# A first unit of 254 tokens, a load on ScalarE's queue and a new order of the steps, in a fused attention and gated feed-forward kernel

## The chip, the core and the metric

One NeuronCore of a Trainium2 chip runs the whole program. The metric is the time of one execution on the device in microseconds (us), the median of several runs. Engines are named as the profile names them: PE is TensorE (the matrix engine; PEld its loads of stationary operands), ACT is ScalarE, DVE is VectorE, POOL is GpSimd, SP is SyncE, which here only starts transfers (DMAs).

## The reference

Chunked attention over 64-token chunks, followed by a feed-forward layer with a depthwise convolution over three neighbouring tokens as its gate. B=8, H=8, S=576, D=64, so the model width is 512; the inner width is 1024.

```python
scores = scale * q_c @ k_c.T            # inside each chunk of 64 tokens
attn = exp(scores - max(scores)); attn = attn / (sum(attn) + 1e-09)
x = (attn @ v_c)  ->  (B, S, 512)
h = maximum(x @ w_in, 0)                # (B, S, 1024)
conv_out[s] = cw[0] * h[s-1] + cw[1] * h[s] + cw[2] * h[s+1]   # zero beyond a sequence's ends
out = (h * sigmoid(conv_out)) @ w_out
```

q, k and v are float32; w_in, conv_w and w_out are float64.

## The kernel before, in words

The tokens of all sequences stand in one line of 4608. Attention works on 36 tiles of 128 tokens (two chunks each), the feed-forward on 16 units, two for each sequence of 576 tokens: 288 and 288.

Attention of a tile t (function `att`): load q and k (`load_rows` for tiles 0 to 8, in groups of three tiles after that), load v, turn q and k so that the head dimension lies on the partitions (`t_pe`, two steps on PE, each copied out of PSUM by ACT in `t_copy`), the scores (PE), row maximum and subtraction (DVE), exponential (ACT), row sum and reciprocal (DVE), the scaling (POOL, `s_norm`), turning the probabilities (`p_pe` on PE, `p_copy` on ACT), the product with v (`attn_v`), and the result split into a rounded part `x_h` (ACT) and the rest `x_l` (DVE). For tiles below `NP` = 5 a row of `load_rows` carries two tokens and is 512 bytes long, and a `t_pe` step is eight matmuls at line 177; for tiles 5 to 8 a row is one token of 256 bytes and a step is four transposes at line 182. Tiles 0 to 8 share two places for their rows (`qk_103` and `qk_104` in the order below), and from tile 12 on the turning of q, k and the probabilities is done without PE.

Feed-forward of a unit u: eight blocks f of 128 inner columns. `mm1` (line 360) multiplies x with w_in in three products (x_h by the rounded weights, x_l by the rounded weights, x_h by the rest), 12 matmuls that stream the unit's tokens plus the neighbours that the convolution needs (290 columns). Then ACT takes the ReLU (`h_relu`) and the middle tap (`c_mid`), DVE adds the outer taps, ACT the tanh (`c_sig`), DVE the product, ACT the rounded part (`g_hi`) and POOL the rest (`g_lo`). `mm2` (line 414) is for an output tile t of 128 tokens and a block f: three matmuls of 512 columns; eight of these steps make a tile, which ACT copies out (`o_copy`) and SP stores (`o_store`). A unit's `mm1` needs x of every attention tile that its tokens touch: unit 0 with 290 columns needs tiles 0, 1 and 2. An output tile needs all units that it touches.

The float64 weights are split on the chip: `w_load` brings a quarter of a matrix (or half of that) into one of two places (`w_105`, `w_106`), then `w_scale` (ACT), `w_shift` and `w_words` (DVE; after these the place is free), `w_hi` (ACT), and `w_left_g` (POOL). A block of `mm1` needs the pieces of its two f, an `mm2` step those of its f.

What runs when is written out: every step is recorded with an engine, a cost and its buffers, `order_` is a list of step numbers, a small planner gives each step a start by its booked cost, and the steps are emitted by that start. Each engine runs its instructions in that order, and waits only for data and buffers. In front of PE steps with an early start the kernel puts filler matmuls on `ident` (lines 926 and 929), which compute nothing that is used; how many is worked out from `pe_free`, the time that the planner books for each filler, and `SLACK`.

```python
while idle and pe_free + (2.0 if pe_free < 5.0 else 1.0) < begin[i] - SLACK:
    nc.tensor.matmul(banks[idle[-1]], lhsT=ident, ...)        # 128x512
```

## Time and profile before

| | |
|---|---|
| runs | 492.12 us median of three (491.23 to 492.7) |
| the profiled execution | 490.69 us, of which the span from first to last instruction is 488.9 us |
| busy, share of the span | PE 98%, DVE 70%, ACT 61%, POOL 39% |
| first `mm1` matmul, last `mm2` matmul on PE | 31.60 us, 485.11 us |
| first `mm2` matmul | 57.82 us |
| moved by DMA | 50.16 MB |

The page gives busy times, the span in 40 slices with a digit for the busy tenths of each, the chain of work that ended last, groups of instructions, and DMA issues. Idle time of an engine costs only where the chain runs through it. Matmuls overlap, so the mean duration of one is longer than the distance between two starts; where the text gives the cost of a matmul it is the distance.

### The profile page before, as it was taken

Reading aid. Unit: us, or ns where it says so; the run is one execution under the profiler, and the core shown is the slowest. Engines: PE = TensorE matmul, PEld = TensorE weight load, DVE = VectorE, ACT = ScalarE, POOL = GpSimd, SP = SyncE. Lnnn points to the kernel's source line nnn. Section 1 sums busy time; section 2 is a strip of 40 time slices with the busy share of each in tenths; the row PEclk is TensorE's granted clock in tenths of the full one; section 3 lists DMA queues with packets and bytes.
Section 4 is the critical chain, followed back from the end, with each engine's and each line's share of the span. In section 5 each row is a group of like instructions: output and inputs, shape, how many; then the busy total and the mean of one; then the engine's idle time right before and its main releaser. Section 6 shows DMA issues by size and latency. Waiting matters only on the chain.

```text
span 488.9 us, 12846 instructions
## 1 busy us (share of the span) xinstructions
PE 478.4 (98%) x4961; PEld 425.2 (87%) x4961; DVE 342.6 (70%) x726; ACT 299.2 (61%) x749; POOL 192.0 (39%) x261
## 2 busy tenths in 40 slices
PE   7799999999999999999999999999999999999996
PEld 4689899989899889898898999998889899998885
DVE  3789988767877788888778687978786655563300
ACT  4589997667564656765556566655654566565411
POOL 1245565252351635355242525352523155143120
PEclk9899999999999999999999999999999999999999
DMA  8998955234655744266565444547302002010012
GB/s 214 297 271 214 269 96 81 48 49 89 131 114 112 147 84 98 47 143 131 101 132 101 100 79 76 118 95 165 82 23 83 24 6 66 0 44 1 21 66 86
DMA packets 180610, 50.16 MB, mean 103 GB/s; under 512 B 164653, under 2 KB 172869, under 8 KB 180549
## 3 DMA queue, kind: packets, MB, share of 16 engines
...
q14 instruction: 23, 0.18, 0.1%
...
## 4 chain that ended last, share of the span: by engine, by line
PE 90%; DMA 4%; ACT 2%; DVE 2%; POOL 1%; issue 1%; SPq 0%; POOLq 0%; ACTq 0%
PE b_ps L414 42%; PE b_ps L360 39%; DMA qk<-in_k 3%; PE sx_ps L309 2%; PE sx_ps L226 2%; PE b_ps L177 2%; PE z_ps L309 1%; DMA w<-in_moe_w_out 1%; PE z_ps L226 1%; PE b_ps L295 1%; DVE wt L456 1%; POOL wi_l L460 1%; ACT wt L447 0%; ACT c L372 0%; SPq L121 0%
## 5 line engine op out<-in xcount | busy, mean ns | idle before, releaser
L405 POOL TENSOR_TENSOR g_l<-c,g_h 128x288 fp32r<-128x288 f32 (+8 forms) x184 | 110.1, 620 | 184.9 <-ACT g_h L401 155.6
L414 PE MATMUL b_ps<-wo_h,g_h 128*128 128x512 f32 x288 | 115.6, 402 | 0.0
L414 PE MATMUL b_ps<-wo_h,g_l 128*128 128x512 f32 x288 | 113.6, 394 | 0.0
L414 PE MATMUL b_ps<-wo_l,g_h 128*128 128x512 f32 x288 | 113.4, 394 | 0.0
L376 DVE SCALAR_TENSOR_TENSOR c<-b_ps,cw,c 128x287 f32<-128x287 f32 (+1 forms) x128 | 64.7, 509 | 55.1 <-ACT c L372 54.7
L360 PE MATMUL b_ps<-x_h,wi_h 128*128 128x290 f32 x512 | 90.3, 298 | 0.2 <-ACT qkT L195 0.2
L360 PE MATMUL b_ps<-x_l,wi_h 128*128 128x290 f32 x512 | 89.6, 297 | 0.0
L367 ACT ACTIVATE b_ps<-b_ps 128x290 f32<-128x290 f32 x128 | 50.8, 399 | 63.1 <-PE b_ps L360 62.8
L360 PE MATMUL b_ps<-x_h,wi_l 128*128 128x290 f32 x512 | 89.2, 296 | 0.0
L360 PEld LDWEIGHTS b_ps<-x_h,wi_h 128*128 128x128 f32 x512 | 80.2, 189 | 9.2 <-ACT qkT L195 0.4
L391 DVE SCALAR_TENSOR_TENSOR c<-c,b_ps 128x288 f32<-128x288 f32 x128 | 56.7, 446 | 35.7 <-ACT c L388 35.2
L388 ACT ACTIVATE c<-c 128x288 f32<-128x288 f32 x128 | 56.6, 444 | 41.0 <-DVE c L382 40.1
L360 PEld LDWEIGHTS b_ps<-x_l,wi_h 128*128 128x128 f32 x512 | 75.8, 190 | 0.0
L360 PEld LDWEIGHTS b_ps<-x_h,wi_l 128*128 128x128 f32 x512 | 75.4, 189 | 0.0
L372 ACT ACTIVATE c<-b_ps,cw 128x288 f32<-128x288 f32 x128 | 63.9, 501 | 9.7 <-POOL g_l L405 2.4
L382 DVE SCALAR_TENSOR_TENSOR c<-b_ps,cw,c 128x288 f32<-128x288 f32 (+1 forms) x128 | 64.8, 512 | 2.8
L414 PEld LDWEIGHTS b_ps<-wo_h,g_l 128*128 128x128 f32 x288 | 54.2, 188 | 12.7
L401 ACT CAST g_h<-c 128x288 fp32r<-128x288 f32 (+8 forms) x184 | 58.3, 355 | 7.1 <-PE b_ps L414 3.6
L414 PEld LDWEIGHTS b_ps<-wo_h,g_h 128*128 128x128 f32 x288 | 54.4, 189 | 8.6
L414 PEld LDWEIGHTS b_ps<-wo_l,g_h 128*128 128x128 f32 x288 | 54.2, 188 | 7.5
L271 POOL TENSOR_TENSOR wt<-wt,z 128x512 f32<-128x512 f32 x24 | 25.3, 1053 | 45.9 <-DVE z L262 18.6
L419 ACT ACTIVATE wt<-b_ps 128x512 f32<-128x512 f32 x36 | 21.4, 597 | 31.2 <-PE b_ps L414 31.1
...
## 6 DMA issues: line engine op xcount, KB each, us to landing
out<-wt SPq DMA_DIRECT2D x36, 256.0 KB, 2.4
v<-in_v SPq DMA_DIRECT2D x21, 256.0 KB, 3.5
...
wt<-wt SPq DMA_DIRECT2D x48, 64.0 KB, 2.0
...
```

The lines of the kernel that those rows point to most:

```text
L271: nc.gpsimd.tensor_tensor(out=two(st, "to"), in0=two(st, "of"), in1=z, op=ALU.mult)
L360: nc.tensor.matmul(h_ps[:, 0:hi - lo], lhsT=wt[:, f // 2, kt, P * (f % 2):P * (f % 2) + P], rhs=xt[:, u % NX, kt, 0:hi - lo], start=n == 0 ...
L367: nc.scalar.activation(out=h, in_=h, func=AF.Relu)
L372: nc.scalar.mul(out=st["c"], in_=banks[st["h"]][:, i0:i0 + st["n"]], mul=cw[:, FT + f:FT + f + 1])
L376: nc.vector.scalar_tensor_tensor(out=c[:, a:n], in0=banks[st["h"]][:, i0 + a - 1:i0 + n - 1], scalar=cw[:, f:f + 1], in1=c[:, a:n], op0=AL ...
L382: nc.vector.scalar_tensor_tensor(out=c[:, 0:b], in0=banks[st["h"]][:, i0 + 1:i0 + 1 + b], scalar=cw[:, 2 * FT + f:2 * FT + f + 1], in1=c[: ...
L388: nc.scalar.activation(out=st["c"], in_=st["c"], func=AF.Tanh, scale=0.5)
L391: nc.vector.scalar_tensor_tensor(out=st["c"], in0=st["c"], scalar=1.0, in1=banks[st["h"]][:, st["i0"]:st["i0"] + st["n"]], op0=ALU.add, op ...
L401: nc.scalar.copy(out=g_h[:, f, gs], in_=st["c"][:, cs])
L405: nc.gpsimd.tensor_tensor(out=g_l[:, f, gs], in0=st["c"][:, cs], in1=g_h[:, f, gs].bitcast(F32), op=ALU.subtract)
L414: nc.tensor.matmul(banks[st["o"]], lhsT=gt[:, f, o:o + P], rhs=wt[:, f, :], start=f == 0 and n == 0, stop=f == FT - 1 and n == 2)
L419: nc.scalar.mul(out=st["os"], in_=banks[st["o"]], mul=0.5)
```

## The change

- **Units.** The first sequence is cut into 254 and 322 tokens instead of 288 and 288; the other sequences stay. Unit 0 then streams 256 columns and needs attention tiles 0 and 1 alone; unit 1 streams 324. `x_h` and `x_l` get slots of differing length (`x_slot`), the buffer `c` is longer. Output tile 1 (tokens 128 to 255) now touches units 0 and 1.
- **Loads.** `NP` = 7: tiles 5 and 6 are loaded two tokens to a row and turned by the eight matmuls. Tile 0's q and k are issued from ACT's queue, ahead of ACT's table load.
- **The last output tile** is made in two halves of 256 columns, each with its own eight `mm2` steps, copy and store.
- **Filler.** A filler is booked with 1.5 and then 0.9 us instead of 2.0 and 1.0, `SLACK` is 0.3 instead of 0.7, PE counts as free from 1.4 us.
- **Buffers.** `e` has two buffers instead of three.
- **The list** `order_` is a new one.

```diff
-    CUTS0 = [0, HS]
-    XU = HS + 2
-    XS = XU + 2
+    FIRST = 2 * P - 2
+    CUTS0 = [0, FIRST]
+    NC_ = S - FIRST
     NX = 3
+    XS = [HS + 4, NC_ + 2, HS + 4]
...
-    SLACK = 0.7
-    NP = 5
+    SLACK = 0.3
+    NP = 7
...
-                    nc.sync.dma_start(out=r[i, p0:p0 + n], ...)
+                    (nc.sync if t else nc.scalar).dma_start(out=r[i, p0:p0 + n], ...)
...
-        st["e"] = work3.tile([P, H, C], F32, name="e")
+        st["e"] = work.tile([P, H, C], F32, name="e")
...
+    def x_slot(x, u):
+
+        o = KT * sum(XS[0:u % NX])
+        return x[:, o:o + KT * XS[u % NX]].rearrange("p (k i) -> p k i", k=KT)
...
-    def mm2(st, t, f):
+    def mm2(st, t, f, m=slice(0, DM)):
...
-            nc.tensor.matmul(banks[st["o"]], lhsT=gt[:, f, o:o + P], rhs=wt[:, f, :],
+            nc.tensor.matmul(banks[st["o"]][:, m], lhsT=gt[:, f, o:o + P], rhs=wt[:, f, m],
...
+            cuts = [(slice(0, DM),), ] if t < NT - 1 else [(slice(0, DM // 2),), (slice(DM // 2, DM),)]
...
-        0, 30, 12, 72, 91, 31, 32, 33, 13, 1, 14, 77, 15, 73, 16, 36, 74, 75, 2, 4, 17, 3, 92, 76, 110, 5, 6,
...
-    pe_free, until_ = 2.0, 110.0
+    pe_free, until_ = 1.4, 110.0
+    ahead = next(i for i in order_ if steps[i]["fn"] is load_rows)
+    steps[ahead]["fn"](*steps[ahead]["args"])
+    nc.scalar.activation(out=rebias, in_=ident[:, 0:1], func=AF.Exp)
+    nc.gpsimd.memset(rebias, -896.0 * 2 ** 23)
...
-            while idle and pe_free + (2.0 if pe_free < 5.0 else 1.0) < begin[i] - SLACK:
+            while idle and pe_free + (1.5 if pe_free < 5.0 else 0.9) < begin[i] - SLACK:
```

How the order moves is shown at three places. A row is a line, an operation, the tile written and those read, and a count.

First PE, from the middle of the start-up to the first `mm1`. L177 (after: L176) is `t_pe`, L226 (L225) the scores, L295 (L294) `p_pe`, L309 (L308) the product with v, L360 (L364) `mm1`, L929 (L941) filler, L507 the turning of conv_w. Before:

```order
L177 MATMUL b_ps<-ident,qk_104 64x128 x8
L295 MATMUL b_ps<-ident,e 128x128 x4
L309 MATMUL sx_ps<-pT,v 64x64 x32
L507 MATMUL b_ps<-ident,wt 128x24
L177 MATMUL b_ps<-ident,qk_103 64x128 x8
L295 MATMUL b_ps<-ident,e 128x128 x4
L226 MATMUL sx_ps<-qkT 64x64 x16
L309 MATMUL sx_ps<-pT,v 64x64 x16
L177 MATMUL b_ps<-ident,qk_103 64x128 x8
L929 MATMUL b_ps<-ident 128x128
L360 MATMUL b_ps<-x_h,wi_h 128x290 x4
```

and after, the same engine and place:

```order
L294 MATMUL b_ps<-ident,e 128x128 x8
L941 MATMUL b_ps<-ident 128x128 x2
L225 MATMUL sx_ps<-qkT 64x64 x16
L308 MATMUL sx_ps<-pT,v 64x64 x16
L176 MATMUL b_ps<-ident,qk_101 64x128 x16
L308 MATMUL sx_ps<-pT,v 64x64 x16
L176 MATMUL b_ps<-ident,qk_102 64x128 x16
L364 MATMUL b_ps<-x_h,wi_h 128x256 x4
```

Before, tile 2's `p_pe` and product with v stand ahead of the first `mm1`; after, those of tiles 0 and 1 alone do, but both `t_pe` steps of tiles 4 and 5 (`qk_101`, `qk_102`), of which tile 5's stood behind it before.

Second the start of the loads, on SP (before):

```order
L434 DMA w_105<-in_moe_w_in 128x2x512
L434 DMA w_106<-in_moe_w_in 128x2x512
L121 DMA qk_103<-in_q 64x8x128
L121 DMA qk_103<-in_k 64x8x128
L121 DMA qk_104<-in_q 64x8x128
L121 DMA qk_104<-in_k 64x8x128
L434 DMA w_105<-in_moe_conv_w 24x256
```

and after, SP's queue (tile 0 is issued by ACT):

```order
L438 DMA w_103<-in_moe_conv_w 24x256
L120 DMA qk_102<-in_q 64x8x128
L120 DMA qk_102<-in_k 64x8x128
L438 DMA w_104<-in_moe_w_in 128x2x512
L438 DMA w_103<-in_moe_w_in 128x2x512
L120 DMA qk_101<-in_q 64x8x128
L120 DMA qk_101<-in_k 64x8x128
```

Tiles 0 and 1 now go ahead of the first two half pieces of w_in, which went ahead of them before; the last two rows are tile 2.

Third SP at the first pieces of w_out, up to the second of them, which holds blocks 0 and 1 and with that what the first `mm2` step needs. Before:

```order
L434 DMA w_105<-in_moe_w_in 128x4x512
L128 DMA qk_104<-in_q 128x8x64
L128 DMA qk_104<-in_k 128x8x64
L434 DMA w_106<-in_moe_w_out 128x2x1024
L167 DMA v<-in_v 128x4x64
L167 DMA v<-in_v 64x4x64 x2
L434 DMA w_105<-in_moe_w_out 128x2x1024
```

and after:

```order
L438 DMA w_103<-in_moe_w_in 128x4x512
L166 DMA v<-in_v 128x4x64
L166 DMA v<-in_v 64x4x64 x2
L438 DMA w_104<-in_moe_w_out 128x2x1024
L127 DMA qk_102<-in_q 128x8x64
L127 DMA qk_102<-in_k 128x8x64
L166 DMA v<-in_v 64x4x64 x4
L438 DMA w_103<-in_moe_w_out 128x2x1024
```

Ahead of that second piece stood q and k of tiles 0 to 5 and v of tiles 0 to 3; now q and k of tiles 0 to 7 and v of tiles 0 to 4, two tiles of 0.52 MB and one v of 0.26 MB more. Behind the first `mm2` step PE now has blocks of `mm1` of units 1 and 2 where steps of output tile 1 stood, since that tile waits for unit 1.

More of the change, by code (lines that the diff above doesn't have):

```diff
@@ L90, in attn_ffn @@
     rebias = const.tile([P, 1], F32, name="rebias")
-    nc.scalar.activation(out=rebias, in_=ident[:, 0:1], func=AF.Exp)
-    nc.gpsimd.memset(rebias, -896.0 * 2 ** 23)
     wi_h = const.tile([P, FT // 2, KT, 2 * P], F32R, name="wi_h")
@@ L97, in attn_ffn @@
     wo_l = const.tile([P, FT, DM], F32R, name="wo_l")
-    x_h = const.tile([P, NX, KT, XS], F32R, name="x_h")
-    x_l = const.tile([P, NX, KT, XS], F32R, name="x_l")
+    x_h = const.tile([P, KT * sum(XS)], F32R, name="x_h")
+    x_l = const.tile([P, KT * sum(XS)], F32R, name="x_l")
     g_h = const.tile([P, FT, GR], F32R, name="g_h")
@@ L553, in att @@
             r = "wslot" if t in W_ROWS else "slot"
[L554 removed]
+            ld = step("SP", 0.02 if t == 0 else 1.2 if (2 * t) % NCK < NCK - 1 else 2.3, load_key, load_rows, (st, t), take=[(r, st)], lag=1.8 if t < NP else 2.6)
             tt = []
@@ L721, in attn_ffn @@
         for i, t in enumerate(outs_in[u] if u <= NU - 1 else []):
-            st = {}
+            cuts = [(slice(0, DM),), ] if t < NT - 1 else [(slice(0, DM // 2),), (slice(DM // 2, DM),)]
             prev = None
-            for f in range(FT):
-                key = U[u + 1] + (U[u + 2] - U[u + 1]) * (i + f / FT) / len(outs_in[u]) + 0.3
-                units = [v_ for v_ in range(NU) if UNITS[v_][0] < P * t + P and P * t < UNITS[v_][1]]
-                prev = step("PE", 0.7, key, mm2, (st, t, f), [prev] + wo_done[f] + [g_done[v_, f] for v_ in units],
-                            take=[("bk", st, "o")] if f == 0 else [])
-                mm2_of[t, f] = prev
-            s = step("ACT", 0.6, key + 1, o_copy, (st,), [prev], take=["wt"], free=[("bk", "o")])
-            step("SP", 0.5, key + 2, o_store, (st, t), [s], free=["wt"], lag=0.8)
+            for n, m in enumerate(cuts):
+                st, w = {}, 1.0 / len(cuts)
+                m = m if w < 1.0 else ()
+                for f in range(FT):
+                    key = U[u + 1] + (U[u + 2] - U[u + 1]) * (i + f / FT) / len(outs_in[u]) + 0.3 + 3.0 * n
+                    units = [v_ for v_ in range(NU) if UNITS[v_][0] < P * t + P and P * t < UNITS[v_][1]]
+                    prev = step("PE", 0.018 + 0.682 * w, key, mm2, (st, t, f) + m, [prev] + wo_done[f] + [g_done[v_, f] for v_ in units],
+                                take=[("bk", st, "o")] if f == 0 else [])
+                    mm2_of[t, f] = prev
+                s = step("ACT", 0.18 + 0.42 * w, key + 1, o_copy, (st,) + m, [prev], take=["wt"], free=[("bk", "o")])
+                step("SP", 0.5, key + 2, o_store, (st, t) + m, [s], free=["wt"], lag=0.8 * w)
     early = {"DVE": 0.083, "ACT": 0.092, "PE": 0.0, "POOL": -0.075, "SP": -0.05}
@@ L932, in attn_ffn @@
         n = len(nc.cur_bb.bb.instructions) if steps[i]["port"] else 0
-        steps[i]["fn"](*steps[i]["args"])
+        if i != ahead:
+            steps[i]["fn"](*steps[i]["args"])
         if steps[i]["port"]:
```

27 lines of the change are left out of this document (13 added, 14 removed), and 242 rows, old and new, of the table order_.

## The prediction

> **What bounds the kernel now.** I read the page first, then busy time by stretch, then the timeline of the start and the chain of waits. The page's 40 slices are 12.2 us each.
>
> ```profile
> span 488.9 us, 12846 instructions
> PE   7799999999999999999999999999999999999996
> DMA  8998955234655744266565444547302002010012
> ```
>
> PE is full from the third slice to the last but one, and DMA is full in the first five slices. Busy time by stretch (the stretch, its length, busy us and instructions of PE, PEld, DVE, ACT, POOL, then the granted clock, the DMA share and GB/s):
>
> ```profile
> 18.00:31.60 13.60, 12.83 (x270) 10.91 (x270) 9.64 (x19) 9.81 (x19) 6.02 (x5) 0.87 0.91 250
> 31.60:45.00 13.40, 13.40 (x162) 12.65 (x166) 13.06 (x28) 12.27 (x24) 6.50 (x5) 1.00 0.96 256
> 45.00:60.00 15.00, 14.75 (x244) 13.44 (x241) 14.10 (x31) 14.26 (x33) 9.06 (x7) 1.00 1.05 260
> 60.00:80.00 20.00, 20.00 (x187) 18.40 (x187) 17.01 (x36) 18.10 (x45) 11.82 (x11) 1.00 0.54 95
> ```
>
> After 31.60 PE has nothing to give: 0.25 us idle up to 80, and full slices after that. So the time is the start of the dense run, plus PE's work from there, plus the tail. But from 31.60 to 80 ACT is busy 44.63 of 48.40 us (12.27 + 14.26 + 18.10), 92%: an earlier start must be fed by an engine with 3.8 us to spare. The start on PE:
>
> ```profile
> 8.67 2.98 PE L177 MATMUL b_ps<-ident,qk 128*64 128x128 f32 x48 [1.62 <-DMA qk<-in_k]
> 17.88 4.40 PE L177 MATMUL b_ps<-ident,qk 128*64 128x128 f32 x48 [2.37 <-DMA qk<-in_k]
> 31.60 0.78 PE L360 MATMUL b_ps<-x_h,wi_h 128*128 128x290 f32 x4
> ```
>
> PE waits for rows of q and k twice, 1.62 and 2.37 us, and begins `mm1` at 31.60. On ACT and DVE, x of tiles 0 and 1, and then of tile 2:
>
> ```profile
> 26.67 1.07 ACT L345 CAST x_h<-sx_ps 128x512 fp32r<-128x512 f32 x2 [0.23 <-PE sx_ps L309]
> 30.60 0.73 ACT L345 CAST x_h<-sx_ps 128x136 fp32r<-128x136 f32 x3 [0.27 <-PE sx_ps L309]
> 27.78 1.29 DVE L349 TENSOR_TENSOR x_l<-sx_ps,x_h 128x512 fp32r<-128x512 f32 x2 [0.88 <-ACT x_h L345]
> ```
>
> The rounded x of tiles 0 and 1 stood at 27.74; unit 0 waited another 3.9 us for tile 2's.
>
> **The start of the dense run.** Two ways to the new time of the first `mm1`.
>
> First by shift. Bytes moved early:
>
> ```profile
> 1.00:4.00 3.00, 2.64 (x3) 1.17 (x4) 0.00 (x0) 1.23 (x2) 0.39 (x2) 1.00 0.60 155
> 4.00:7.00 3.00, 3.00 (x6) 1.05 (x4) 0.89 (x2) 0.94 (x2) 0.00 (x0) 1.00 1.05 337
> ```
>
> That is 0.47 MB by 4.0 and 1.48 by 7.0. Tile 0 lay behind two half pieces of w_in, so 3 x 0.52 = 1.57 MB had to pass, at the same rate reached at 7.3; PE began at 8.67, 1.3 later. Now tiles 0 and 1 go first, 1.07 MB with conv_w: reached at 5.8, so both have landed by 7.1, and tile 0 a little sooner, say 6.5. That is 2.1 us earlier than 8.67. With the same time from there to x_h of tile 1, `mm1` begins at 31.6 - 3.9 - 2.1 = 25.6.
>
> Second by what now stands ahead of it. Both `t_pe` steps of tile 5 are the last thing before `mm1`. Ahead of tile 5's landing stand six tiles (3.15 MB), 2.1 MB of w_in, two v (0.52): 5.8 MB. Before, 0.222 x 8 + 0.280 x 10 = 4.58 MB had passed by 18.0 (rows below), and 0.250 MB per us after that gives 5.8 MB at 22.9, plus 1.3 for landing 24.2. Its sixteen matmul rows twice take 2.07 us (the chain's first row below), so `mm1` begins at 26.3.
>
> ```profile
> 0.00:8.00 8.00, 5.69 (x8) 2.23 (x8) 1.65 (x4) 2.83 (x4) 0.80 (x7) 1.00 0.77 222
> 8.00:18.00 10.00, 6.61 (x137) 5.61 (x139) 7.00 (x15) 6.15 (x10) 2.58 (x2) 1.00 1.00 280
> ```
>
> The second is the later one and so the one that counts. I take 26.6, with 25.6 as the early end and 28.0 as the late one (tile 5 landing another 1.4 late, or the clock below): **5.0 us earlier**.
>
> **PE's work from there on.** Costs from the chain of waits (start, us, what, count):
>
> ```profile
> 8.67 2.07 PE b_ps L177 x32
> 60.74 1.63 PE b_ps L360 x12
> 62.36 0.44 PE b_ps L182 x4
> 68.55 0.44 PE b_ps L295 x4
> 71.24 0.47 PE sx_ps L309 x32
> 461.30 23.81 PE b_ps L414 x102
> 485.14 0.60 ACT wt L419
> ```
>
> A matmul of 290 columns costs 1.63 / 12 = 0.136 us, one of 512 costs 23.81 / 102 = 0.233; a line through both gives 0.00044 per column and 0.121 for 256. Units of 256 and 324 columns stream as many as 290 and 290, so `mm1` is unchanged by that line; no row shows a 256-column matmul, and if it cost as much as one of 290 (the dearest end) it would be 96 x 0.015 = 1.4 us more. What moves across the first `mm1`: tile 5's two `t_pe` go ahead of it (-0.88), tile 6's two become eight-matmul steps (2.07 - 0.88 = +1.19), tile 2's `p_pe` and product with v now come behind it (+0.44 + 0.47). The last tile's halves: 48 x 0.121 - 24 x 0.233 = +0.2. Sum: **+1.4 us** of PE work. The filler costs nothing where PE would wait anyway; its cover is the wait for tile 0, and the new filler (two of 512 columns and five of 128) is shorter than the old one, so it ends before the tile has landed.
>
> **Waits that may come.** The first `mm2` step needs the second piece of w_out. Before:
>
> ```profile
> 35.47 0.37 SPq L434 DMA_DIRECT2D w<-in_moe_w_out  x1
> 42.14 1.16 ACT L447 ACTIVATE wt<-w 128x1024 f32<-128x1024 f32 x1
> 46.79 4.82 POOL L460 TENSOR_TENSOR wo_l<-wt,wo_h 128x1024 fp32r<-128x1024 f32 x2 [2.60 <-ACT c L372]
> 57.82 0.47 PE L414 MATMUL b_ps<-wo_h,g_h 128*128 128x512 f32 x1
> ```
>
> It landed at 42.14 and was split by 51.61 (9.5 us), 6.2 us before its use. Now 1.31 MB more stand ahead of it, 5.1 us at 0.256 MB per us: landed 47.2, split by 56.7 at the old pace, by 53.7 if POOL takes it at once (1.16 of ACT, some 2 of DVE, 1 of ACT, 2.4 of POOL). PE had 57.82 - 31.60 = 26.2 us between first `mm1` and first `mm2`; now some 28, since one block more stands between them: 26.6 + 28.0 = 54.6. So the wait lies between 0 and 2.1; I take **0.5**, nearer the low end because POOL does both pieces in 4.82 and the first is done early. What queues behind it is all of PE's work. The other queues that a step is moved past (v, the stores) have slack of several us and cost nothing while PE is the bound.
>
> `e` with two buffers costs nothing while a subtraction comes after the `p_pe` two tiles before, which the order has everywhere in the start; without that, DVE's queue stands for one `p_pe`, 0.44.
>
> The ACT side as a second bound. Ahead of its first ReLU ACT now has, by the order, one full `w_scale`, one half `w_hi` and one tile's x_h fewer; one `p_copy` fewer and one q,k copy more are alike, each a 128x512 copy out of PSUM.
>
> ```profile
> L447 ACT ACTIVATE wt<-w 128x1024 f32<-128x1024 f32 x6 | 7.0, 1160 | 1.6 <-DMA w<-in_moe_w_out 1.0 <-DMA w<-in_moe_w_in 0.6
> L492 ACT CAST wi_h<-wt 128x512 fp32r<-128x512 f32 x4 | 2.5, 631 | 1.2 <-DVE wt L456 1.2
> ```
>
> 1.16 + 0.63 + 0.54 (half of the 1.07 above) = 2.3 us of work that ACT still owes when it starts on the ReLUs 5 us earlier. If ACT sets the pace to 80 us the gain is 5.0 - 2.3 = 2.7; by PE's side it is 5.0 - 1.4 - 0.5 = 3.1. The two agree, which is why I trust the size.
>
> **The tail.** The last copy is of 256 columns instead of 512, an estimated 0.40 instead of 0.60 (x_h pieces of 136 columns took 0.73 / 3 = 0.24 above), and the last store is half as long. By the page's issue rows a 256 KB store lands after 2.4 us and a 64 KB transfer after 2.0, so about 0.25 is saved there.
>
> ```profile
> out<-wt SPq DMA_DIRECT2D x36, 256.0 KB, 2.4
> wt<-wt SPq DMA_DIRECT2D x48, 64.0 KB, 2.0
> ```
>
> Together **-0.45**, bounds 0 and -0.6.
>
> Sum: -5.0 + 1.4 + 0.5 - 0.45 = **-3.55 us**. The profiled execution took 490.69, which gives 487.1; the median of the runs shown stands 1.4 above it at 492.12, so the predicted median is 488.6. About 0.3% (1.5 us) is what a measurement of this kernel can tell from no change.
>
> **The clock, row against rule.** By stretch, around PE's second wait:
>
> ```profile
> 16.00:17.80 1.80, 0.00 (x0) 0.00 (x0) 1.80 (x6) 0.92 (x2) 0.00 (x0) 1.00 1.07 297
> 20.00:21.00 1.00, 1.00 (x13) 1.00 (x11) 0.61 (x2) 0.40 (x1) 0.59 (x2) 0.50 1.03 204
> 23.00:25.00 2.00, 2.00 (x24) 1.64 (x24) 1.86 (x4) 1.06 (x2) 0.00 (x0) 1.00 0.84 217
> ```
>
> After 2.37 us without work the granted clock was 0.50 at 20 to 21, and 48 matmuls took 4.40 instead of 2.98. With the loads of tiles 2 to 5 again one place at a time, a gap of that length can come back, and then the run of transposes ahead of `mm1` (two tiles, 4.1 us) takes half as long again, +2. The Trainium skill (TensorE: Matmul & The Clock Gate, Part 1) says that the clock falls to half after an idle window of about 3.4 us and needs as long of sustained work to come back; the windows run free of the program. By that rule the shorter filler and the gaps here, each under 2.4 us, would leave the clock whole and the sum as it stands; by the row a 2.4 us gap is enough and the sum would be 2 us smaller in gain. The trace bears the half rate out and not the length, so the cold case stays among the rivals.
>
> **The rivals.** A block of `mm1` asks of ACT, by line (line, operation, shapes, count, busy us, mean ns, idle before):
>
> ```profile
> L372 ACT ACTIVATE c<-b_ps,cw 128x288 f32<-128x288 f32 x128 | 63.9, 501 | 9.7 <-POOL g_l L405 2.4 <-ACT b_ps L367 0.4
> L388 ACT ACTIVATE c<-c 128x288 f32<-128x288 f32 x128 | 56.6, 444 | 41.0 <-DVE c L382 40.1
> L367 ACT ACTIVATE b_ps<-b_ps 128x290 f32<-128x290 f32 x128 | 50.8, 399 | 63.1 <-PE b_ps L360 62.8
> L401 ACT CAST g_h<-c 128x288 fp32r<-128x288 f32 x72 | 29.9, 427 | 4.0 <-PE b_ps L414 3.4 <-DVE c L391 0.5
> ```
>
> - *Given back* (no measurable change). The clock falls to half ahead of `mm1` (+2.0) and the wait for w_out is the full 2.1 (+1.6): -3.55 + 3.6 = 0, 492.2; with one of them and the dearer 256-column matmul (+1.4) some -0.3, 491.8. For it: each has a row behind it, and the 3.8 us of slack on ACT won't make up for both. Against: they needn't meet, and ACT had another 3.8 us idle in 18.00 to 31.60, which the new order uses.
> - *PE short of work that ACT needn't feed* (slower). Output tile 1 now waits for unit 1, so only tile 0's eight `mm2` steps (8 x 0.70 = 5.6 us) can stand between the blocks of `mm1`, where two tiles' stood. PE asks 5.6 us sooner for blocks: 3.4 of them, each 0.50 + 0.44 + 0.40 + 0.43 = 1.77 of ACT, 6.1 us. With none of it fitting in, the sum is -3.55 + 6.1 = +2.5: 494.7. It decides from 5.1 us of such waiting on. Against: 3.8 us of it has room, and further steps of tiles 2 and 3 soon follow.
> - *More* (gain over 5.0). `mm1` at 25.6, no wait for w_out, and PE's 0.25 us of idle in 45 to 60 gone too: -6.0 + 1.4 - 0.45 - 0.25 = -5.3: 486.8. For it: the shift of the loads alone gives 25.6. Against: tile 5's transposes stand in the way.
>
> **How the numbers follow.** Forecast (gain 1.5 to 5.0) 0.62, more 0.11, given back 0.18, slower 0.09. Faster 0.73, same 0.18, slower 0.09. The likeliest case reaches from 487.1 (start at 25.6, no wait: -6.0 + 1.4 - 0.45) to 491.1 (start at 27.5, 2.1 of wait: -4.1 + 1.4 + 2.1 - 0.45). The range takes in half of "more" and the given-back case: 486.2 to 492.0.
>
> **What would show it.** Right: the first `mm1` between 25.6 and 28.0 with tile 5's transposes right ahead of it, first `mm2` near 54.6, PE without idle rows after that, the last PE matmul near 482, the end 3.3 after it. Wrong: `mm1` at 29 or later (a late tile 5, or a clock of 0.50 before it); PE idle rows released by ACT between 30 and 80; 256-column matmuls that cost as much as 290; a first `mm2` that waits for POOL's `wo_l`.

## The result, and the profile after

The changed kernel takes 497.11 us (median of 4 runs, 496.27 to 497.88) against 492.18 of the kernel before (4 runs): a ratio of 1.0102, 95% interval 1.0076 to 1.0127. It is 5 us slower, where 3.5 us faster was forecast. The profiled execution took 496.27, its span 494.5.

The page of the changed kernel, the same three lines (slices of 12.4 us), and with them the granted clock:

```profile
span 494.5 us, 12995 instructions
PE   7789999999999999999999999999999999999997
PEclk9879999999999999999999999999999999999999
DMA  6879965333564645346676343457122003010102
```

PE is still full to the end, but now only from the fourth slice on, and the DMA line, which was 8998955 in the first seven slices, begins 6879965. The clock of PE is below full in slices 2 and 3. Busy time by stretch (PE, PEld, DVE, ACT, POOL, clock, DMA share, GB/s):

```profile
8.00:18.00 10.00, 8.38 (x152) 7.46 (x147) 7.23 (x13) 5.25 (x9) 2.32 (x2) 0.84 0.72 198
18.00:31.60 13.60, 10.49 (x206) 9.20 (x203) 6.33 (x13) 7.55 (x12) 3.68 (x3) 0.75 0.81 227
31.60:45.00 13.40, 13.25 (x226) 11.83 (x222) 11.86 (x24) 11.80 (x27) 5.62 (x5) 0.99 0.97 273
45.00:60.00 15.00, 14.50 (x218) 13.52 (x218) 12.87 (x26) 13.31 (x29) 7.33 (x6) 1.00 0.87 226
```

From 8 to 18 the DMA share fell from 1.00 to 0.72, from 18 to 31.6 from 0.91 to 0.81, and in that stretch PE, DVE and ACT all do less than before. After 31.6 PE is nearly full again. The start on PE (start, us, what, count, idle before it and its releaser):

```profile
7.00 2.94 PE L176 MATMUL b_ps<-ident,qk 128*64 128x128 f32 x48 [1.57 <-DMA qk<-in_k]
14.65 3.63 PE L176 MATMUL b_ps<-ident,qk 128*64 128x128 f32 x32 [1.58 <-DMA qk<-in_k]
18.38 2.06 PE L176 MATMUL b_ps<-ident,qk 128*64 128x128 f32 x32
26.10 1.13 PE L308 MATMUL sx_ps<-pT,v 64*64 64x64 f32 x32 [2.62 <-ACT pT L299]
27.17 3.68 PE L176 MATMUL b_ps<-ident,qk 128*64 128x128 f32 x32
31.84 2.06 PE L176 MATMUL b_ps<-ident,qk 128*64 128x128 f32 x32
33.83 0.74 PE L364 MATMUL b_ps<-x_h,wi_h 128*128 128x256 f32 x4
```

Tile 0's transposes begin 1.67 us earlier (7.00 against 8.67) and tile 2's 3.2 earlier (14.65 against 17.88), but the first `mm1` comes 2.2 us later, at 33.83 (31.60 before, 26.6 forecast). Two of the four runs of 32 transposes take 3.63 and 3.68 and not 2.06: the clock, which was granted at 0.50 there (rows further down).

Three points of the dense run tell where the 5.9 us at the last matmul lie (485.11 before, 491.04 now): first `mm1` +2.2, from there to the first `mm2` +3.6 (26.22 before, 29.83 now), from there to the last matmul nothing (427.3 and 427.4). The first `mm2` in the timeline, and the end of the chain of waits:

```profile
63.66 0.50 PE L418 MATMUL b_ps<-wo_h,g_h 128*128 128x512 f32 x1
467.18 23.86 PE b_ps L418 x126
```

After the last matmul it now takes 494.5 - 491.04 = 3.46 to the end, 3.79 before.

Why the loads fall behind shows on SP (its DMA issues in order of time; the second fence is its longest wait, with total, times, longest):

```profile
2.73 2.23 SPq L438 DMA_DIRECT2D w<-in_moe_w_in  x2
9.07 0.61 SPq L120 DMA_DIRECT2D qk<-in_q  x1
...
13.22 0.62 SPq L120 DMA_DIRECT2D qk<-in_q  x1
...
14.62 0.56 SPq L438 DMA_DIRECT2D w<-in_moe_w_in  x1
18.32 1.27 SPq L120 DMA_DIRECT2D qk<-in_q  x2
...
24.50 0.62 SPq L120 DMA_DIRECT2D qk<-in_q  x1
```

```profile
SPq L120 <- PE b_ps L176: 9.9, 3, 4.0
```

The rows are tiles 2, 3, the third piece of w_in, and tiles 4 and 5. SP has issued everything that it has a place for by 4.96 and then stands for 4.0 us until PE has transposed tile 0 and its place is free. It stands again for 3.1 us ahead of tile 4, until tile 2 is transposed, and for 2.8 us ahead of tile 6. Tile 5's rows come in the queue behind tile 4's and three issues of v, and are asked for at 24.50. The prediction had them landed at 24.2.

On ACT, the scaling of the third piece of w_in waits for its landing and stands ahead of the copies of p that PE waits for:

```profile
24.45 1.12 ACT L451 ACTIVATE wt<-w 128x1024 f32<-128x1024 f32 x1 [3.34 <-DMA w<-in_moe_w_in]
25.47 1.07 ACT L299 COPY pT<-b_ps 128x512 f32<-128x512 f32 x2
```

So there were four suspects: the order of the loads, ACT's order, the clock, and the PE work of the two-token tiles.

### The profile page after: what moved, and what is told of

It is laid out like the page before. It is cut to its first block, busy times and chain, and to the rows that moved or that the text cites. A ratio compares the mean times of both kernels' runs of the same rounds, so it can differ in the third digit from the quotient of the medians.

```text
span 494.5 us, 12995 instructions
## 1 busy us (share of the span) xinstructions
PE 482.3 (98%) x5033; PEld 430.4 (87%) x5033; DVE 342.8 (69%) x726; ACT 298.7 (60%) x750; POOL 190.2 (38%) x261
## 4 chain that ended last, share of the span: by engine, by line
PE 89%; DMA 4%; ACT 2%; DVE 1%; SPq 1%; POOL 1%; issue 1%; ACTq 0%; DVEq 0%
PE b_ps L418 41%; PE b_ps L364 39%; PE sx_ps L308 3%; DMA w<-in_moe_w_in 2%; PE sx_ps L225 2%; PE z_ps L308 1%; DMA w<-in_moe_w_out 1%; PE b_ps L176 1%; PE z_ps L225 1%; DMA qk<-in_k 1%; PE b_ps L294 1%; POOL g_l L409 1%; SPq L166 1%; SPq L120 1%; ACT wt L451 0%
## 5 line engine op out<-in xcount | busy, mean ns | idle before, releaser
L409 POOL TENSOR_TENSOR g_l<-c,g_h 128x288 fp32r<-128x288 f32 (+10 forms) x184 | 108.4, 613 | 186.4 <-ACT g_h L405 169.1
L418 PE MATMUL b_ps<-wo_h,g_h 128*128 128x512 f32 (+1 forms) x296 | 117.5, 397 | 0.0
L418 PE MATMUL b_ps<-wo_h,g_l 128*128 128x512 f32 (+1 forms) x296 | 115.0, 388 | 0.0
L418 PE MATMUL b_ps<-wo_l,g_h 128*128 128x512 f32 (+1 forms) x296 | 114.8, 388 | 0.0
L380 DVE SCALAR_TENSOR_TENSOR c<-b_ps,cw,c 128x288 f32<-128x288 f32 (+3 forms) x128 | 64.7, 509 | 49.8 <-ACT c L376 49.2
L364 PE MATMUL b_ps<-x_h,wi_h 128*128 128x290 f32 (+2 forms) x512 | 90.5, 299 | 0.1
L364 PE MATMUL b_ps<-x_l,wi_h 128*128 128x290 f32 (+2 forms) x512 | 89.2, 296 | 0.0
L364 PE MATMUL b_ps<-x_h,wi_l 128*128 128x290 f32 (+2 forms) x512 | 89.1, 296 | 0.0
L364 PEld LDWEIGHTS b_ps<-x_h,wi_h 128*128 128x128 f32 x512 | 79.6, 189 | 9.0 <-DVE c L395 0.7
L364 PEld LDWEIGHTS b_ps<-x_l,wi_h 128*128 128x128 f32 x512 | 75.6, 189 | 0.0
L364 PEld LDWEIGHTS b_ps<-x_h,wi_l 128*128 128x128 f32 x512 | 75.2, 189 | 0.0
L376 ACT ACTIVATE c<-b_ps,cw 128x288 f32<-128x288 f32 (+2 forms) x128 | 63.3, 500 | 8.3 <-POOL g_l L409 2.2
L386 DVE SCALAR_TENSOR_TENSOR c<-b_ps,cw,c 128x288 f32<-128x288 f32 (+3 forms) x128 | 65.2, 512 | 2.7
L405 ACT CAST g_h<-c 128x288 fp32r<-128x288 f32 (+10 forms) x184 | 57.7, 357 | 10.6 <-DVE c L395 6.4
```

The lines of the kernel that those rows point to most:

```text
L364: nc.tensor.matmul(h_ps[:, 0:hi - lo], lhsT=wt[:, f // 2, kt, P * (f % 2):P * (f % 2) + P], rhs=x_slot(xt, u)[:, kt, 0:hi - lo], start=n = ...
L376: nc.scalar.mul(out=st["c"], in_=banks[st["h"]][:, i0:i0 + st["n"]], mul=cw[:, FT + f:FT + f + 1])
L380: nc.vector.scalar_tensor_tensor(out=c[:, a:n], in0=banks[st["h"]][:, i0 + a - 1:i0 + n - 1], scalar=cw[:, f:f + 1], in1=c[:, a:n], op0=AL ...
L386: nc.vector.scalar_tensor_tensor(out=c[:, 0:b], in0=banks[st["h"]][:, i0 + 1:i0 + 1 + b], scalar=cw[:, 2 * FT + f:2 * FT + f + 1], in1=c[: ...
L405: nc.scalar.copy(out=g_h[:, f, gs], in_=st["c"][:, cs])
L409: nc.gpsimd.tensor_tensor(out=g_l[:, f, gs], in0=st["c"][:, cs], in1=g_h[:, f, gs].bitcast(F32), op=ALU.subtract)
```

## The experiments

All runs at a glance; times in us, each ratio against runs of the kernel before on the same chip; the last three columns are from each run's profile. Where the text compares two runs "by the ratios", it takes the difference of these ratios, since the runs were not all on one chip. In e1, e6, e9, e10, e13, e14 and e16 to e18 the kernel puts in filler only up to a planned start of 20.5 us (110 in the changed kernel); their traces show as many fillers ahead of the first `mm1` as that of the changed kernel, and none behind it. In e8 and e11 (21 us) one filler of 128 columns is gone that the kernel before has.

| run | median | ratio, 95% | first `mm1` | first `mm2` | last matmul |
|---|---|---|---|---|---|
| before | 492.1 to 492.7 | 1 | 31.60 | 57.82 | 485.11 |
| after | 497.11 | 1.0102 (1.0076 to 1.0127) | 33.83 | 63.66 | 491.04 |
| e1 ACT's order | 495.7 | 1.0057 (1.0026 to 1.0088) | 33.41 | 63.20 | 491.1 |
| e2 filler | 494.93 | 1.0033 (1.0006 to 1.0060) | 31.80 | 62.12 | 488.9 |
| e3 weights first | 498.15 | 1.0117 (1.0047 to 1.0186) | 36.97 | 64.22 | 492.0 |
| e4 before, NP 7 | 495.62 | 1.0067 (1.0040 to 1.0094) | 32.59 | 60.80 | 489.1 |
| e5 after, NP 5 | 496.01 | 1.0088 (1.0062 to 1.0113) | 33.62 | 64.06 | 494.2 |
| e6 `mm1` ahead | 508.07 | 1.0334 (1.0303 to 1.0365) | 33.67 | 73.17 | 502.4 |
| e7 before, filler | 492.94 | 1.0026 (1.0010 to 1.0042) | 31.85 | 58.37 | 485.7 |
| e8 before, cut, block moved | 498.32 | 1.0134 (1.0106 to 1.0162) | 30.36 | 61.16 | 493.2 |
| e9 third place, 3 `wt` | 534.0 | 1.0855 (1.0814 to 1.0897) | 27.61 | 58.23 | 529.5 |
| e10 the same, ACT's order | 534.44 | 1.0861 (1.0820 to 1.0901) | 28.25 | 57.89 | 528.8 |
| e11 before, cut | 497.11 | 1.0101 (1.0072 to 1.0129) | 32.39 | 59.14 | 491.2 |
| e12 before, two `e` | 493.6 | 1.0019 (0.9998 to 1.0039) | 32.05 | 60.01 | 488.2 |
| e13 place in `c` | 492.89 | 1.0016 (0.9991 to 1.0041) | 28.56 | 59.71 | 489.1 |
| e14 the same, NP 5 | 494.38 | 1.0036 (1.0009 to 1.0062) | 26.13 | 58.97 | 489.3 |
| e15 before, place in `c` | 496.37 | 1.0070 (1.0042 to 1.0098) | 32.44 | 60.40 | 492.0 |
| e16 e14, ACT's order | 494.33 | 1.0036 (1.0014 to 1.0059) | 26.36 | 59.62 | 489.4 |
| e17 place, own `c` | 491.38 | 0.9984 (0.9968 to 1.0000) | 27.11 | 56.70 | 484.2 |
| e18 e17, NP 6 | 493.44 | 1.0012 (0.9991 to 1.0033) | 27.53 | 60.53 | 488.2 |

**e1, ACT's order.**

```
order_ (ACT): ... w_scale(third piece), p_copy(0), p_copy(1) ...
          ->  ... p_copy(0), p_copy(1), w_scale(third piece) ...
```

> The changed kernel with one step moved on ACT: the scaling of the third w_in piece (1 MB) goes behind the copies of p of tiles 0 and 1, which it stood ahead of; nothing else moves. Theory (the start is held by ACT's in-order queue behind that piece's landing at 24.4, and after that by the piece's own split, whose low part was ready at 32.6 while `mm1` needs it 1.4 us after its first matmul): the copies run at about 22 instead of 25.5, the product with v of tile 0 follows at once, the first `mm1` comes at 31.2 to 32.0 (33.83 in the changed kernel), and the time falls by about 2.0 to 495.1. Rival 1 (the two transposes of tile 5 are the last bound, as the prediction had it: landed at 28.2 plus 2.07): first `mm1` at 30.3, 493.6. Rival 2 (the queue on ACT is not what holds PE): 497.1, first `mm1` still near 33.8.

The first `mm1` came near where rival 2 had it, at 33.41. The time is 1.4 us less by the medians and 2.2 by the ratios, with intervals that overlap. The copies ran early and the product with v of tile 0 with them, at 22.15, but PE's next work then waited 3.98 us for tile 4's rows, and the clock fell again:

```profile
26.81 3.68 PE L176 MATMUL b_ps<-ident,qk 128*64 128x128 f32 x32 [3.98 <-DMA qk<-in_k]
```

ACT's wait was one of two that end at about the same time; the other is the rows of tile 4.

**e2, filler in the wait.**

```
+ if the step is attn_v of tile 0: three matmuls of ident, 128x512, into a free bank
```

> The changed kernel with three more filler matmuls of 512 columns on PE right ahead of the product with v of tile 0, in the 2.62 us in which PE waited for ACT; nothing else moves. Theory (part of the loss is the clock, granted 0.50 from 26 to 32 after that gap): the clock is 1.0 from 26 on, tile 4's sixteen-matmul pair takes 2.06 instead of 3.68, the first `mm1` comes some 1.6 to 2.2 earlier, at 31.6 to 32.2, no earlier because the third w_in piece's low part is ready only at 32.6; time 495.2. Rival (the filler only moves the wait, because rows of tile 5 land late): first `mm1` within 0.5 of 33.8, time 497.1 or, if the filler delays the product with v, 497.6.

As the theory said, in place and size. Tile 4's transposes take 2.06, and the first `mm1` comes 2.0 us earlier; the time fell by 2.2 by the medians (3.4 by the ratios). The mean granted clock was 0.999 or more in all ten executions, and 0.990 to 0.995 in the four of the changed kernel:

```profile
22.05 2.84 PE L938 MATMUL b_ps<-ident 128*128 128x512 f32 x6
26.28 0.69 PE L308 MATMUL sx_ps<-pT,v 64*64 64x64 f32 x32 [1.39 <-ACT pT L299]
26.91 2.06 PE L176 MATMUL b_ps<-ident,qk 128*64 128x128 f32 x32
31.80 0.74 PE L364 MATMUL b_ps<-x_h,wi_h 128*128 128x256 f32 x4
```

**e3, weights first again.** The first part of the order (up to the first `mm1`) is that of the kernel before, with its filler; the rest is as changed.

> The changed kernel with the start-up order of the kernel before up to the first `mm1` (two half pieces of w_in ahead of tile 0, all loads on SP, the old filler); the cut at 254, the two-token loads up to tile 6, the order after the start and the last tile's halves stay as changed. Theory (the new load order is what made the start late): first `mm1` at 31.6 give or take 0.7, as in the kernel before, first `mm2` some 29.8 later at 61.4, time 494.9: better than the changed kernel by 2.2 and still worse than the kernel before by the 1.4 of PE work and the block more ahead of the first `mm2`. Rival 1 (the cut at 254 with tile 5's transposes ahead of `mm1` costs it, whatever the load order): first `mm1` at 33 to 34, time 497. Rival 2 (nothing but the start counts): 492.3.

My theory was that tiles before weights made the start late. It fell: with the old load order the time is no better (the intervals overlap), and the first `mm1` came another 3.1 us later, with tile 5's rows the last thing waited for:

```profile
35.01 2.03 PE L178 MATMUL b_ps<-ident,qk 128*64 128x128 f32 x32 [0.51 <-DMA qk<-in_k]
36.97 0.74 PE L366 MATMUL b_ps<-x_h,wi_h 128*128 128x256 f32 x4
```

So it isn't tiles before weights. In both load orders the changed kernel has tiles 4 and 5 transposed ahead of `mm1`, and a place for their rows comes free only as earlier rows are done with.

**e4, two-token loads alone, in the kernel before.**

```
-    NP = 5
+    NP = 7
```

> The kernel before with only the two-token loads extended from tiles 0 to 4 to tiles 0 to 6, its own order kept. In that order both tiles' transposes stand behind the first `mm1`. Theory (PE is full there, so its work counts in full): 4 steps of 1.03 instead of 0.44, +2.4 us, 494.5, first `mm1` unchanged at 31.6, first `mm2` some 2.4 later at 60.2. Rival 1 (the longer rows make the transfers shorter and that gives it back): within 0.5 of 492.2. Rival 2 (the loads of tile 5 land late in either form and only tile 6 counts): +1.2, 493.4.

3.3 us slower by the ratio, where 2.4 was worked out. In the profile the first `mm1` is 1.0 later and the stretch to the first `mm2` 28.21 long and not 26.22, 2.0 more. The work of the sixteen-matmul steps is paid in full where PE is full.

**e5, two-token loads undone in the changed kernel.** `NP = 5` again.

> The changed kernel with the two-token loads undone for tiles 5 and 6 (again tiles 0 to 4 only), the order kept. Theory (the sixteen-matmul transposes of these two tiles are PE work that nothing hides: the run of them alone in the old order cost 3.3 us of time): four steps of 0.44 instead of 1.03, 2.4 us less PE work, 1.2 of it ahead of the first `mm1`, which comes at 32.6; time 494.7. Rival (tile 5's rows land later in the one-token form, and PE waits for them instead): first `mm1` at 33.8 or later, only tile 6's share is won, 495.9.

1.1 us less than the changed kernel by the medians, 0.7 by the ratios, with intervals that overlap. Tile 4's rows came at 27.88 and the clock was half; behind that PE had waits that it didn't have with NP 7. The rival is nearer, but the whole of the 2.4 us did not turn up here, while e4 had it in full the other way.

**e6, the first two blocks ahead.**

```
first two blocks: f 4 and 5 -> f 0 and 1 (half pieces loaded first swapped to suit)
attn_v(0), attn_v(1), x of tiles 0 and 1, mm1 f 0 and 1  -> ahead of t_pe of tile 4
w_scale(third piece) -> behind x_h of tile 1
```

> The changed kernel with its first two `mm1` blocks made those of f 0 and 1 (their half pieces of w_in are loaded first in place of those of f 2 and 3) and put ahead of the transposes of tiles 4 and 5, the third piece of w_in scaled behind x of tile 1, and both products with v ahead of tile 3's scores; loads, cut, two-token loads and tail as changed. Theory (the late start is made by what stands between x of tile 1 and the first `mm1`: rows of tile 4 that land at 25 to 27 behind the 1 MB piece, two tiles' transposes, and that piece's split): first `mm1` at 25.0 to 26.0, both blocks (2.9 us) lie in the wait for tile 4, the clock stays whole, and the transposes of tile 5 end near 32; that is worth 33.8 + 2.9 - 32 = 4.6 against the changed kernel: 492.5. Rival 1 (ACT and the splits can't feed an earlier start; what is won ahead is lost as waits before 60): first `mm1` as early, 495. Rival 2 (x or the half pieces' splits aren't ready): first `mm1` at 29 or later, 496.

508: my own order made a worse wait. The product with v of tile 1 stood ahead of tile 4's transposes on PE, but v of tile 1 stands behind tile 4's rows on SP, and these wait for a place:

```profile
26.72 1.50 PE L308 MATMUL sx_ps<-pT,v 64*64 64x64 f32 x32 [3.04 <-DMA v<-in_v]
32.61 1.13 PE L225 MATMUL sx_ps<-qkT 64*64 64x64 f32 x32 [4.39 <-DVE x_l L353]
```

It tells nothing of the idea, only that SP's queue must be moved together with PE's.

**e7, the kernel before with filler in its own wait.**

```
+ if the step is t_pe(0) of tile 2: 18 matmuls of ident, 128x128, into a free bank
```

> The kernel before with 18 more filler matmuls of 128 columns (0.107 us each, 1.9 us) in PE's second wait, ahead of the transposes of tile 2; nothing else. Theory (a wait of 2.4 us without work is enough to halve the clock, and the run of 48 transposes that follows then takes 4.4 instead of 2.98): the run takes 2.98, first `mm1` at 30.2 instead of 31.6, time 1.4 less: 491.1. Rival 1 (the start is held by the landing of tiles 3 and 4 or by x of tile 2, and PE only waits there instead): first `mm1` within 0.4 of 31.6, time unchanged at 492.5. Rival 2 (the filler stands in the way of rows that have landed): 493.

Rival 1. The clock was 1.00 throughout and the run of 48 transposes took 2.96. My price for the filler was wrong (each of the 18 took 0.24, not 0.107), so it ran past the landing and put that run off by 1.8 us. Still the first `mm1` moved by only 0.25:

```profile
14.90 4.29 PE L926 MATMUL b_ps<-ident 128*128 128x128 f32 x36
19.66 2.96 PE L177 MATMUL b_ps<-ident,qk 128*64 128x128 f32 x48
27.38 1.13 PE L177 MATMUL b_ps<-ident,qk 128*64 128x128 f32 x16 [0.36 <-DMA qk<-in_k]
31.85 0.78 PE L360 MATMUL b_ps<-x_h,wi_h 128*128 128x290 f32 x4
```

PE waited 0.36 us for tile 4's rows, so in this run the start hangs on them and on x of tile 2. It does not show that the cold stretch of the kernel before is free: the filler put PE off by more than the whole clock saved (1.8 us against 1.4), and with it tile 4's rows, whose place comes free behind these transposes (asked for at 21.75; 20.60 before). The plain executions of the kernel before point the other way. Of the 107 timed beside the experiments, 15 had a mean granted clock of 0.998 or more, and their median is 490.4 us; that of the other 92 is 492.6. Whether the clock made the 15 shorter, or earlier rows made both, is not separated.

**e8 and e11, the cut in the kernel before; e12, its buffers.** e8 and e11 set `FIRST = 2 * P - 2` and `e` in two buffers in the kernel before; e8 moves the first block of `mm1` up as well. e12 has the two buffers alone.

> The kernel before with the cut at 254 alone (unit 0 needs x of tiles 0 and 1 only) and the first `mm1` block moved up behind tile 2's p transposes, ahead of the product with v of tile 2 and of half of tile 4's transposes; `e` in two buffers as in the change, to make room; loads, two-token tiles and tail as before. Theory (the cut by itself is worth the stretch that PE waits for x of tile 2, and no more): first `mm1` at 28.5 to 29.5, no more than the 1.0 us of idle and filler between 28 and 31.6 is won, 0.3 to 1.0 better: 491.8. Rival 1 (the cut alone is the loss: shorter blocks ask more of ACT, whose fixed cost for one block stays): 1 to 2.5 worse, 494. Rival 2 (the cut is worth the whole 3.9 us that the prediction gave it): 489.

> The kernel before with the cut at 254 and nothing else but `e` in two buffers: no block is moved. Theory (the loss of 6 us in the run of the cut with a moved block came from the moved block, which stood ahead of rows of tile 4 that were late anyway, and from an order that was not made for it): first `mm1` near 31.6, first `mm2` later by the block more that stands ahead of it and by half a us, time 492.5 to 494. Rival (blocks of 324 columns and of 254 each cost PE or ACT more than two of 290): slower by 4 or more, with idle rows of PE behind 60, 497.

> The kernel before with `e` in two buffers instead of three, nothing else. The prediction took this to cost nothing. Theory: 492.2, within 0.5. Rival (DVE's queue stands for a `p_pe` where a subtraction comes early, and ACT and PE wait behind it): 1 to 4 slower.

e8: 6 us slower, so rival 1's sign with more than its size. The block came earlier, at 30.36, but into a stretch where PE first waits 2.39 us for tile 4's rows and then runs at half the clock:

```profile
27.69 1.98 PE L178 MATMUL b_ps<-ident,qk 128*64 128x128 f32 x16 [2.39 <-DMA qk<-in_k]
30.36 1.20 PE L366 MATMUL b_ps<-x_h,wi_h 128*128 128x256 f32 x4
```

e11 shows that the moved block is not it: the cut with two `e` costs 4.9 us, as its rival said, of which e12's two buffers explain 0.9 by the ratios (from nothing to 1.9 by e12's interval). In e11 the stretch from 80 to 120, which was full before, has 1.8 us of idle PE, and 31.6 to 45 has 1.5:

```profile
31.60:45.00 13.40, 11.89 (x159) 11.09 (x156) 12.13 (x25) 11.51 (x20) 6.39 (x5) 1.00 1.04 270
80.00:120.00 40.00, 38.19 (x391) 32.59 (x392) 26.43 (x57) 24.39 (x65) 13.66 (x23) 1.00 0.33 54
```

The changed kernel has neither (13.25 and 40.00). So it may be the order: one made for units of 288 need not fit units of 254 and 322. How much of e11 is the cut and how much the unfitting order, these runs can't tell.

**e9 and e10, a third place for rows of q and k.**

```
-    slots = [... for i in range(2)]        -    work4 (wt): bufs=4
+    slots = [... for i in range(3)]        +    work4 (wt): bufs=3
```

> The changed kernel with a third place for rows of q and k (4 KB for each partition, made free by having three instead of four buffers for the split halves and output rows); order of the start unchanged. Theory (the loads, not the engines, set the start, and they are starved: with weights behind tiles 0 and 1, SP waits 9.9 us in three waits for a place of q and k, and the DMA share is 0.72 from 8 to 18 where it was 1.00): the rows of tile 2 are asked for at once, DMA share 8 to 18 at 0.95 or more, the third w_in piece lands by 19 instead of 24.4, tile 4 by 21 to 22, first `mm1` at 26 to 29, time 491 to 493. Rival 1 (the transfers are as slow with more of them under way; bytes and not places are the bound): first `mm1` within 1 of 33.8, 497. Rival 2 (the start comes earlier, but what stands behind it, ACT's and the splits' work, gives it back by 60): first `mm1` at 26 to 29, first `mm2` after 62, 496.

> The same with the scaling of the third w_in piece put behind the copies of p of tiles 0 and 1 on ACT, as in the run of that step alone. Theory: once the rows of tile 4 come early, ACT's order counts for what it didn't there: first `mm1` another 0 to 1.5 earlier than with the third place alone, but not before 25 (the piece's low part), time the same to 1.5 less. Rival (ACT's order never counts): as the third place alone, within 0.5.

The start came as the theory said, 6.2 us earlier, with the engines of the DMA full; the price, a buffer less for split halves and output rows, was far more than I had allowed for, 22 us of idle PE between 120 and 300 alone:

```profile
8.00:18.00 10.00, 8.44 (x176) 7.44 (x173) 7.20 (x13) 6.28 (x12) 2.33 (x2) 1.00 1.10 305
120.00:200.00 80.00, 69.37 (x766) 61.08 (x765) 53.32 (x116) 40.11 (x107) 27.23 (x37) 0.96 0.50 101
200.00:300.00 100.00, 88.40 (x948) 77.11 (x947) 70.00 (x147) 51.20 (x132) 36.70 (x51) 0.95 0.46 92
```

ACT's order makes no difference to the time here (e10 against e9, 0.4 apart).

**e13 to e16, the place at no price.** Tile 2's rows go into memory that the block buffers `c` use from the first block on. In these four the seven `c` are handed out in turn, and the kernel leaves out the wait for the last reader of one, so a block's values can be overwritten; the work is the same, the waits need not be.

```
+    c_all = work1.tile([P, 7 * NC_], F32)      # c number i at NC_ * i
+    row_slot(tile 2) = c_all[:, 3 * NC_:3 * NC_ + 1024]
```

> The changed kernel with a place of its own for tile 2's rows of q and k, in memory that is the block buffers `c` later on, so that no other buffer is given up; order as changed. Theory (the loss is the starvation of the loads): DMA share 8 to 18 at 0.95 or more, first `mm1` at 27 to 28.5, first `mm2` near 58.3, PE without idle after 60, the time 5.4 below the changed kernel: 491.7, no better than the kernel before by more than 1, since the PE work of the change stays. Rival 1 (an earlier start is given back behind 60 even without the price in buffers): 494 to 497. Rival 2 (starvation was only part: start as theory, and the prediction's 3.6 of gain appears): 488.6.

> The same with the two-token loads of tiles 5 and 6 undone. Theory (once loads aren't starved, the work of the transposes on PE counts in full): 2.4 us less PE work than with the place alone, 489.3. Rival (the one-token rows are slower to land and PE waits for them, as in the run of NP 5 alone, where 4 us less work gave 1.1 us): within 1 of the place alone, 491.5.

> The kernel before with the same place for tile 2's rows; order as before. Theory (there the DMA engines are busy anyway, 1.00 from 8 to 18, so a place brings little): first `mm1` between 30.5 and 31.9, time 491.2 to 492.5. Rival (the kernel before is starved too: its PE waits 2.37 us for these very rows and its clock falls): first `mm1` at 28 to 29.5, time 489 to 490.

> The changed kernel with the place for tile 2, the two-token loads of tiles 5 and 6 undone, and the scaling of the third w_in piece behind the copies of p on ACT. Theory (with tile 4's rows early, ACT's order counts for 0 to 1): 488.5 to 489.5, first `mm1` at 25.5 to 27. Rival (ACT's order doesn't count, or the piece's own split then comes late): as with the place and NP 5, within 0.5.

e13 recovers 4.2 of the 5 us. e14 and e16 have the earliest `mm1` of all and are no faster than e13: behind it PE idles 4.0 us before the first `mm2` (2.2 in e13). With NP of 5 the median is 1.5 us above e13, with intervals that overlap, where 2.4 below was worked out: the theory falls. The rival's cause falls with it, since behind the first `mm1` PE waits for DVE and ACT and not for rows. e16 is as e14: ACT's order doesn't count here either. e15 brings no earlier start in the kernel before: its DMA engines were full (a share of 1.00 from 8 to 18, 0.96 in e15), and the first `mm1` is at 32.44. Its loss of 3.5 us comes with waits like those of e13 and isn't separated from the way the `c` are handed out.

**e17 and e18, the same place, each `c` handed out when it is free.**

> The changed kernel with a place of its own for tile 2's rows (in the memory of the block buffers `c`, each of which is handed out when it is free, as in the changed kernel). Theory (the loss of 5 us is the starvation of the loads): first `mm1` at 27.5 to 28.7, first `mm2` at 58.2 to 59.2, 427 from there to the last matmul, time 5 us below the changed kernel: 491.5 to 492.5, level with the kernel before. Rival 1 (ACT and DVE bound the stretch to 60 by themselves, so that an earlier start than 28 is worth nothing more): the same time, but with the idle rows of PE between 31 and 60 released by ACT and DVE, 2 us or more in all. Rival 2 (the gain that the prediction saw appears): 488.6.

e17 is the changed kernel without the starvation: 491.38 us, a ratio of 0.9984 to the kernel before, and by the ratios 5.8 us below the changed kernel. Its trace has the same instructions in the same order on every engine as that of the changed kernel, and the same filler. SP, the stretch, PE:

```profile
2.72 2.23 SPq L442 DMA_DIRECT2D w<-in_moe_w_in  x2
5.00 0.61 SPq L123 DMA_DIRECT2D c<-in_q  x1
...
10.29 0.62 SPq L123 DMA_DIRECT2D qk<-in_q  x1
...
19.17 0.62 SPq L123 DMA_DIRECT2D qk<-in_q  x1
```

```profile
8.00:18.00 10.00, 8.94 (x189) 7.71 (x188) 7.70 (x14) 6.75 (x13) 2.34 (x2) 1.00 1.09 305
25.15 2.03 PE L179 MATMUL b_ps<-ident,qk 128*64 128x128 f32 x32 [0.66 <-DMA qk<-in_k]
27.11 0.74 PE L367 MATMUL b_ps<-x_h,wi_h 128*128 128x256 f32 x4
460.36 23.89 PE b_ps L422 x126
```

Tile 2's rows are asked for at 5.00 and not 9.07, tile 5's at 19.17 and not 24.50; the DMA share from 8 to 18 is 1.09, the clock 1.00 all along, and the first `mm1` comes at 27.11. So the one more place gives the whole loss back: it is the starved start, of which the half clock that follows from its waits is a part (2.0 us at the first `mm1` by e2). The gain that the prediction saw doesn't appear (rival 2 falls), and PE's idle time from 31 to 60 is 0.9 and not the 2 of rival 1. The 0.8 us by which e17 is ahead of the kernel before may be the clock alone: all twelve of its executions had a mean clock of 0.999 or more, and the 15 executions of the kernel before at 0.998 or more took 490.4.

> The same with tile 6 back to one-token loads. If PE's work is the bound behind the first `mm1`: two steps of 0.44 instead of 1.03, 1.2 less, 490.5. If ACT and DVE are the bound there: the same 1.2 appears as idle time of PE between 31 and 60, and the time stays within 0.4 of the place alone.

With 1.2 us less work for PE, e18 is 1.4 us slower than e17 by the ratios (2.1 by the medians, on one chip; the intervals overlap a little). From 31.6 to 60 PE has 3.8 us of idle time where e17 has 0.9, ahead of one block most of all, and behind that wait the clock was granted at 0.50 from 39.42 to 42.84:

```profile
39.11 0.98 PE L367 MATMUL b_ps<-x_h,wi_h 128*128 128x256 f32 x4 [2.50 <-ACT qkT L197]
```

Undoing the two-token loads has not paid beyond the noise anywhere in the new order (e5, e14, e18), and making them has cost 3.3 us in the old one (e4).

## Why the prediction was wrong, step by step

The sum was -3.55 us; the span of the profiled execution grew by 5.6. Of the 9.1 us between, 7.2 lie in the start (+2.2 for -5.0), 1.8 in the work behind it (+3.7 for +1.9) and 0.1 in the tail.

- *The bound* (PE full from the start of the dense run on, so the time is that start, the work and the tail) held: the dense part from the first `mm2` is 427 us in before, after and e17.
- *The start by shift.* Tile 0's transposes were to begin 2.1 earlier and began 1.67 earlier.
- *The start by what stands ahead of it* is the step that failed. It counted the bytes up to tile 5's rows and let them flow at the rates of the kernel before, 0.222 and 0.280 MB per us. The rates of a queue that is kept full did not hold in an order in which it ran empty. By 18.0 the changed kernel had moved 0.215 x 8 + 0.198 x 10 = 3.70 MB, not 4.58. I looked at when bytes could arrive and never at when SP could ask for them: two places for q and k, each free only when PE has transposed what lies in it, and weights behind tiles whose place comes free later still. The SP rows above and e17 show it: one more place, and `mm1` is at 27.11, inside the 25.6 to 28.0 that the prediction gave. What stood in its text, "the loads of tiles 2 to 5 again one place at a time", is this very thing; it was used only for the length of PE's waits.
- *The third piece of w_in* was counted in bytes, and its landing left out as something that ACT's queue stands behind. It was asked for at 9.61 before and at 14.62 now, and landed at 24.43, and ACT's queue stood behind that. By e1 this alone moves the first `mm1` by 0.4 us only, because tile 4's rows come as late.
- *The clock.* The rival's case came true as priced: +2.0, and e2 takes back 2.0 at the first `mm1`. The granted clock around the two runs of transposes that took 3.6:

```profile
16.00:18.00 2.00, 2.00 (x22) 1.89 (x18) 2.00 (x3) 0.16 (x1) 1.42 (x2) 0.50 0.97 231
28.00:30.00 2.00, 2.00 (x22) 2.00 (x20) 1.97 (x5) 2.00 (x4) 1.28 (x1) 0.50 0.71 227
```

  A wait of 1.58 and one of 2.62 went ahead of them. The Trainium skill (TensorE: Matmul & The Clock Gate, Part 1) puts the fall to half after an idle window of about 3.4 us, and says that the windows run free of the program. The length of idle time does not agree with these rows. The second half does: the granted clock of the traces changes at steps of 3.41 us alone (the last section has the count).
- *PE's work from the first `mm1` on* was put at +1.4 and the wait for w_out at +0.5. From the first `mm1` to the last matmul before took 453.51, after 457.21, e17 457.12: +3.6 or +3.7. No wait shows at the first `mm2` (0 for the 0.5). (In the kernel before that piece of w_out landed at 41.60; 42.14 is when ACT took it up.) Added up from start to start in the traces, the transposes (+0.4) and `p_pe` (+0.4) came near what was put down. The products with v took +0.9 (+1.1 in e17) for 0.47: the three between the first `mm1` and the first `mm2` took 0.6 to 0.9 each, while the price came from a row behind the first `mm2`. The steps of `mm2` took +0.6 (+0.5) for 0.2, the scores and `mm1` together +0.5 (0 in e17), and idle time, which had no term but the 0.5, +0.8 (+1.2). Why the products with v are dearer early is not shown. So the mended start brings the kernel level, and not 3.5 ahead.
- *256 columns.* Twelve took 1.43, 0.119 each; the line gave 0.121, the dear end 0.136. Right.
- *Two `e` at nothing.* Not shown either way: e12 is 0.2% slower with an interval from 0 to 0.4%.
- *The tail.* 3.46 against 3.79: -0.33 for -0.45. Right in kind.
- *The rivals.* The slower one (PE short of work that ACT needn't feed) has the sign and not the mechanism: PE's idle time from 31.6 to 80 is 0.9 us where it needed more than 5.1. "Given back" had the clock right and the wait for w_out wrong. That the loads could starve stood among no rival (the signs of being wrong name a late tile 5, without a cause), and so the chance of slower, 0.09, was too small.
